# Quarter slots in native float32 for expert remainders of at most 32 tokens, beside 15 full slots

## The chip, the cores and the metric

The kernel runs on one core of a Trainium2 chip. The metric is the device time of one execution in microseconds, the median of several runs. A core has five engines with a queue each: PE (TensorE, matrix products), DVE (VectorE), ACT (ScalarE), POOL (GpSimd) and SP (SyncE, which here only reads control values and issues DMAs). An engine works through its own queue in order and waits on semaphores.

## The reference

Three stages follow each other. Attention with a sigmoid gives a matrix x of 1792 tokens by 768. A mixture of experts sends each token to one of eight experts, by the largest logit. A dense pair of layers with a squared relu ends it.

```python
# attention: 4 batches, 12 heads, 448 positions, 64 per head
attn = 1.0 / (1.0 + np.exp(-(scale * q @ k.T - np.log(S))));  x = attn @ v     # x: 1792 x 768
# experts: w1 is 8 x 768 x 1024, w2 is 8 x 1024 x 768
logits = x @ w_gate
expert_idx = np.argmax(logits, axis=1)
for e in range(8):
    mask = expert_idx == e
    out[mask] = gate_w[mask, None] * (np.maximum(x[mask] @ w1[e], 0.0) @ w2[e])
# dense: w_in is 768 x 2048, w_out is 2048 x 768
h = np.maximum(out @ w_in, 0.0);  result = h * h @ w_out
```

## The kernel before

All numbers are float32. Large products are made of two halves, a high part `h` rounded to the matmul's reduced float32 and the rest `l`: `mm3` issues three matmuls, high by high, high by low and low by high (lines 473 to 476). Attention's second product and the transposes are native float32 matmuls. In attention, two heads of 64 columns run as two column groups of the array, one after the other in program order (line 164).

**Routing** (lines 302 to 345) stands between attention and the experts. DVE finds each token's expert, PE counts tokens per expert and ranks them (`pn`, `prk`), and DVE rounds each count up to a multiple of 128 (`sa`), sums them up (`sx`) and so gives each token a position in a list of slots of 128 rows. `ctl[:,0]` holds the expert of each slot, `ctl[:,1]` whether it differs from that of the slot before (expert 0 for slot 0), `ctl[:,2]` the first row of the slot's result. A product with one-hot matrices (`A`, `Bt`) turns the positions into `idx`, the token of each row of each slot.

**The expert stage** (lines 434 to 640) runs `NBASE` slots, 19, whatever the routing; two more stand in a conditional block behind it. A slot gathers 128 rows of x (`gather`, an indirect DMA on POOL), transposes and splits them (`xtrans`), and goes through eight chunks of weights of 128x1536 (768 KB). Chunks 0 to 3 are `up` (36 matmuls of 512 columns in all), chunks 4 to 7 `down` (48 of 384), with two transposes of the hidden rows (`htrans`) between, and `fin` scales the result by the gate and stores it in `y_d`, with the token's number in a last column.

Weights go through three places. SP loads raw chunks: `reload(s, c)` is a DMA under the condition that the slot's expert differs from the one before, else it is skipped. The raw buffers are filled with expert 0's chunks at the end of attention. ACT then makes the high part `mh[c]` and DVE (POOL for chunk 7) the low part `ml[c]` (`split_m`). `next_chunk(s, c)`, called right after chunk c's matmuls, splits chunk c for slot s+1 and issues `reload(s+2, c)`. So PE is a slot behind the splits and two behind the loads.

The order on each engine is that of the program, written out by hand. For slot 0 the string `FIRST` (line 49) gives it: `h` is a high part on ACT, `l` or `p` a low part on DVE or POOL with `reload(1, c)` behind, `x0` the transposes of slot 0's rows, `r0` the rest of the routing (`late_routing`: first rows, gates' parts `gp`, `Bg`). The gates are one more one-hot product (`gates`, 16 matmuls) after chunk 3 of slot 0, into the PSUM tile `px1` that the second half of the transposes of slot 1 also uses.

The dense stage loads the rows of `y_d` in blocks of 512, the first block during the last expert slots, and scatters its results by token number.

Of the kernel before, what the change touches and what calls it, by code (L numbers as in the profile page):

```python
# [21 lines left out]
NT = B * S  # L22
# [14 lines left out]
NBASE = NTL + 5  # L37
# [19 lines left out]
def moe_kernel(ctx: ExitStack, tc: tile.TileContext, qk, v, wg, wm, w2, out):  # L57
# [8 lines left out]
    y_d = dram.tile([NT + 128, YW], F32, name="y_d")  # L66
    w_d = dram.tile([128, 16, CH], F32, name="w_d")
# [7 lines left out]
    idx = const.tile([128, NSLOT], U32, name="idx")  # L75
    gts = const.tile([128, NSLOT], F32, name="gts")
    ctl = const.tile([128, 3, NSLOT], I32, name="ctl")
    idx2 = const.tile([128, NTL], U32, name="idx2")
    tok = const.tile([128, NSLOT], U32, name="tok")
# [27 lines left out]
    with ExitStack() as actx:  # L107
# [171 lines left out]
        sa, sx = rt([128, 2, 1 + E], "sa"), rt([128, 2, 1 + E], "sx")  # L279
# [5 lines left out]
        A, Bs, Bt = rt([CP, NR, 128], "A", F16), rt([CP, NR, NSLOT], "Bs", F16), rt([CP, NR, NSLOT], "Bt", F16)  # L285
        cmp, r0 = rt([128, NSLOT, E - 1], "cmp"), rt([128, NSLOT], "r0")
        dst_, dd = rt([128, E], "dst_"), rt([128, E - 1], "dd")
        gp, Bg = rt([CP, NR, 3], "gp", BF16), rt([CP, NR, 3, NSLOT], "Bg", BF16)
# [10 lines left out]
        for tile in (ohz[:, :, 0:1], seg[:, :, 0:1], sa[:, :, 0:1], esl[:, 0:1]):  # L299
            nc.gpsimd.memset(tile, 0.0)  # L300
# [18 lines left out]
        V.tensor_scalar(sa[:, 0, 1:], t30, TWO30, None, op0=ALU.subtract)  # L319
        V.tensor_tensor_scan(sx[:, 0], seg[:, 0, :E + 1], sa[:, 0], 0.0, op0=ALU.mult, op1=ALU.add)  # L320
        nc.scalar.activation(sa[:, 1, 1:], pn[:, :E], AF.Copy)
# [7 lines left out]
        V.tensor_copy(ctl[:, 0, :], esl[:, 1:])  # L329
        V.tensor_tensor(ctl[:, 1, :], esl[:, 1:], esl[:, :NSLOT], op=ALU.not_equal)  # L330
# [103 lines left out]
    with ExitStack() as mctx:  # L434
# [4 lines left out]
        ps_ht = mctx.enter_context(tc.tile_pool(name="ps_ht", bufs=1, space=PS, reuse_waits="tile"))  # L439
        ps_y = mctx.enter_context(tc.tile_pool(name="ps_y", bufs=1, space=PS, reuse_waits="tile"))  # L440
# [50 lines left out]
        def make_slot(s, xh, xl, weights):  # L491
            hr = mp.tile([128, 2, 512], F32, tag="hr", name=f"hr_{s}", bufs=1)
# [13 lines left out]
            def up(c):  # L506
# [10 lines left out]
                if c % 2 == 1:  # L517
                    nc.scalar.activation(hr[:, i, :], ps[i], AF.Relu)
# [21 lines left out]

        regs(0)
# [4 lines left out]
        def late_routing():  # L546
            V.tensor_tensor_scan(sx[:, 1], seg[:, 0, :E + 1], sa[:, 1], 0.0, op0=ALU.mult, op1=ALU.add)
# [11 lines left out]
            V.tensor_scalar(ctl[:, 2, :], r0, float(NT), None, op0=ALU.min)  # L559
            V.tensor_tensor(gr, gr, gp[:, :, 1], op=ALU.subtract)  # L560
            V.tensor_copy(gp[:, :, 2], gr)
            for i in range(3):
                nc.gpsimd.tensor_tensor(Bg[:, :, i, :], Bs, gp[:, :, i:i + 1].to_broadcast([CP, NR, NSLOT]), op=ALU.mult)
            for s in range(3):
                row0(s)

        def gates():
            pg = ps_x.tile([128, 4, 128], F32, tag="px1", name="pgt").rearrange("p a b -> p (a b)")
            for t in range(NR):
                nc.tensor.matmul(pg[:, :3 * NSLOT], A[:, t, :], Bg[:, t].rearrange("p a s -> p (a s)"), start=(t == 0), stop=(t == NR - 1))  # L570
            V.tensor_copy(gts, pg[:, :NSLOT])
            V.tensor_tensor(gts, pg[:, NSLOT:2 * NSLOT], gts, op=ALU.add)
            V.tensor_tensor(gts, pg[:, 2 * NSLOT:3 * NSLOT], gts, op=ALU.add)
# [13 lines left out]
        for s in range(NBASE):  # L587
# [16 lines left out]
            for c in range(4, 8):  # L604
# [6 lines left out]
                next_chunk(s, c)  # L611
                if last and c < 7:
# [10 lines left out]
        with tc.If(more < NT):  # L623
            for s in range(NBASE, NSLOT):
# [22 lines left out]
    ps_q = ctx.enter_context(tc.tile_pool(name="ps_q", bufs=1, space=PS, reuse_waits="tile"))  # L647
    for c in range(2, RING):
# [137 lines left out]
```

## Time and profile before

| | us |
|---|---|
| median of 3 runs (1061.55 to 1066.33) | 1066.06 |
| the profiled execution | 1062.08 |
| its span, first to last instruction | 1060.5 |
| PE busy | 1013.8 |
| ACT busy | 638.8 |
| DVE busy | 631.8 |
| POOL busy | 188.4 |

The profile is of one execution. Busy time is the time in which an engine had an instruction running, as a share of the span a mean over all stages. Matmuls overlap each other, so the durations of single matmuls add up to more than their busy time; how fast they run is read from the distance of their starts. Attention lasts until about 185 us, the expert stage from about 205 to 576, the dense stage from 579 to the end. The mean granted clock of TensorE was 0.984.

### The profile page before, as it was taken

How to read it: one execution, taken by the hardware profiler on the slowest of the kernel's cores; microseconds unless marked ns; L12 is line 12 of the kernel's file. 1: busy time of each engine (PE TensorE's matmuls, PEld its weight loads, DVE VectorE, ACT ScalarE, POOL GpSimd, SP SyncE). 2: the span in 40 equal slices, each digit the busy share in tenths (PEclk: the TensorE clock that was granted, in tenths of full speed). 3: DMA queues.
4: the chain of work that ended last, by engine and by line, in shares of the span. 5: the costliest groups of instructions: out<-in, count | busy, mean ns of one | idle time of the engine just before them, and what ended most of it. 6: DMA issues, size and time to landing. Idle time of an engine off the chain costs nothing. (4 is left out here: it accounts for less than half of the span.)

```text
span 1060.5 us, 14396 instructions
## 1 busy us (share of the span) xinstructions
PE 1013.8 (96%) x5502; PEld 857.5 (81%) x5502; DVE 631.8 (60%) x565; ACT 638.8 (60%) x757; POOL 188.4 (18%) x132
## 2 busy tenths in 40 slices
PE   7999999379999999999998999999999999999997
PEld 3555555268888888888887889998899988899997
DVE  3777775788888888888883567433331334323351
ACT  5666664658887888878883664335542255522761
POOL 0000000464253342533411000001000010000100
PEclk9999999689999999999999999999999999999999
DMA  8788988763078174416344547434332432422650
GB/s 281 260 294 298 321 289 295 265 272 134 31 263 303 45 283 170 143 46 218 139 164 151 178 179 260 148 98 128 111 124 95 129 129 90 149 90 90 203 185 30
DMA packets 50104, 187.80 MB, mean 177 GB/s; under 512 B 6576, under 2 KB 17328, under 8 KB 47984
## 3 DMA queue, kind: packets, MB, share of 16 engines
q1 hardware_dynamic: 33872, 155.52, 42.2%
q0 software_dynamic: 4944, 25.56, 6.3%
q10 hardware_dynamic: 11216, 5.75, 2.1%
q8 instruction: 45, 0.74, 0.3%
q14 instruction: 27, 0.22, 0.1%
HBM read 230.85 MB, written 31.47 MB: 247 GB/s over the span
## 5 line engine op out<-in xcount | busy, mean ns | idle before, releaser
L358 DVE TENSOR_TENSOR wl<-raw,wh 128x1536 fp32r<-128x1536 f32 x126 | 256.0, 2053 | 51.8 <-ACT wh L357 49.4
L357 ACT ACTIVATE wh<-raw 128x1536 fp32r<-128x1536 f32 x144 | 213.7, 1484 | 2.9 <-ACT wh L357 0.2
L358 DVE TENSOR_TENSOR wrl<-raw,wrh 128x1536 fp32r<-128x1536 f32 x43 | 75.6, 1758 | 135.4 <-ACT wrh L357 135.4
L476 PE MATMUL py<-wh,hl 128*128 128x384 f32 x304 | 104.9, 345 | 6.0 <-DVE hl L504 6.0
L158 ACT ACTIVATE a<-sc,bias_s 128x896 f32<-128x896 f32 x96 | 82.6, 912 | 44.7 <-PE sc L154 44.5
L474 PE MATMUL py<-wh,hh 128*128 128x384 f32 x304 | 106.9, 352 | 0.0
L475 PE MATMUL py<-wl,hh 128*128 128x384 f32 x304 | 103.3, 340 | 0.1
L714 PE MATMUL pq<-wrh,sh 128*128 128x384 f32 x296 | 100.0, 338 | 0.0
L358 POOL TENSOR_TENSOR wl<-raw,wh 128x1536 fp32r<-128x1536 f32 x18 | 63.9, 3551 | 202.0 <-ACT wh L357 202.0
L716 PE MATMUL pq<-wrh,sl 128*128 128x384 f32 x296 | 99.5, 336 | 0.0
L715 PE MATMUL pq<-wrl,sh 128*128 128x384 f32 x296 | 99.5, 336 | 0.0
L676 PE MATMUL pp<-yh,wrh 128*128 128x512 f32 (+1 forms) x264 | 96.0, 364 | 2.7 <-PEq L623 2.7
L677 PE MATMUL pp<-yl,wrh 128*128 128x512 f32 (+1 forms) x264 | 95.9, 363 | 0.0
L678 PE MATMUL pp<-yh,wrl 128*128 128x512 f32 (+1 forms) x264 | 95.8, 363 | 0.0
L357 ACT ACTIVATE wrh<-raw 128x1536 fp32r<-128x1536 f32 x43 | 63.8, 1484 | 52.5 <-PE pq L716 43.2
L474 PE MATMUL ph<-wh,xh 128*128 128x512 f32 x228 | 92.7, 406 | 0.3 <-ACT xh L460 0.3
L476 PE MATMUL ph<-wh,xl 128*128 128x512 f32 x228 | 90.7, 398 | 0.0
L475 PE MATMUL ph<-wl,xh 128*128 128x512 f32 x228 | 90.6, 398 | 0.0
L680 ACT ACTIVATE r<-pp 128x512 f32<-128x512 f32 (+1 forms) x64 | 34.7, 542 | 86.3 <-PE pp L678 86.3
L358 DVE TENSOR_TENSOR rl<-raw,rh 128x1536 fp32r<-128x1536 f32 x21 | 36.9, 1758 | 75.8 <-ACT rh L357 75.8
L476 PEld LDWEIGHTS py<-wh,hl 128*128 128x128 f32 x304 | 57.8, 190 | 11.5 <-DVE hl L504 11.5
L164 PE MATMUL po<-a,qkv 128*64 128x448 f32 x288 | 64.7, 556 | 0.0
(168 smaller groups left out, 2045.7 us busy)
## 6 DMA issues: line engine op xcount, KB each, us to landing
raw<-in_wm SPq DMA_DIRECT2D x160, 768.0 KB
raw<-w_d SPq DMA_DIRECT2D x62, 768.0 KB
cs<-in_w SPq DMA_DIRECT2D x11, 1536.0 KB
qkv<-in_qk SPq DMA_DIRECT2D x23, 480.0 KB
w_d<-cd POOLq DMA_DIRECT2D x11, 768.0 KB, 9.6
raw<-in_w SPq DMA_DIRECT2D x5, 1536.0 KB
y_d<-y SPq DMA_DIRECT2D x19, 384.5 KB
qkv<-in_v SPq DMA_DIRECT2D x24, 256.0 KB
```

Of the source, the lines that this page charges most:

```text
L158: nc.scalar.activation(a[:, :n], ps[:, :n, :S], AF.Sigmoid, bias=bias_s, scale=1.0 / math.sqrt(D))
L357: nc.scalar.activation(h, src, AF.Copy)
L358: (nc.gpsimd if pool else nc.vector).tensor_tensor(l, src, f32(h), op=ALU.subtract)
L474: nc.tensor.matmul(ps, lh, rh, start=first, stop=False)
L475: nc.tensor.matmul(ps, lh, rl, start=False, stop=False)
L476: nc.tensor.matmul(ps, ll, rh, start=False, stop=last)
L676: nc.tensor.matmul(pp[:, :N], lh, rh, start=(k == 0), stop=False)
L677: nc.tensor.matmul(pp[:, :N], lh, rl, start=False, stop=False)
L678: nc.tensor.matmul(pp[:, :N], ll, rh, start=False, stop=(k == KD - 1))
L714: nc.tensor.matmul(po[t][:, :384], lh, wc[:, o:o + 384], start=(g == 0), stop=False)
L715: nc.tensor.matmul(po[t][:, :384], lh, wcl[:, o:o + 384], start=False, stop=False)
L716: nc.tensor.matmul(po[t][:, :384], ll, wc[:, o:o + 384], start=False, stop=(g == KF2 - 1))
```

## The change

An expert's tokens beyond its full slots, where they are at most 32, no longer get a slot of 128. Up to four such remainders go to quarter slots of 32 rows. The loop of full slots has 15 turns instead of 19, with six in the conditional block behind it. Each quarter is cut in ten events, and `q_due` puts event k right after the chunk with the number 8 + 5k/2, counted over all slots. An event is either a set of transposes (0 and 5) or one chunk of weights, used raw as float32: four column groups of 32, each with its own quarter of the chunk's columns. The weights of a quarter come through two buffers of their own (`qraw`, `QB` = 2), loaded on SP without condition. Routing gets the counts and positions for it, and slot 0 may start with another expert than 0. Some buffers become single: `xh`, `xl`, `hr` (now half as large), `y`, and the PSUM tile `pht`.

```diff
-NBASE = NTL + 5
+NBASE = NTL + 1
+NQ = 4
+QM = 32
+NCOL = NSLOT + NQ
+QB = 2
...
-        V.tensor_scalar(sa[:, 0, 1:], t30, TWO30, None, op0=ALU.subtract)
+        V.tensor_scalar(full, t30, TWO30, None, op0=ALU.subtract)
+        V.tensor_scalar(t30, pn[:, :E], 63.5 - QM, TWO30, op0=ALU.add, op1=ALU.add)
+        V.scalar_tensor_tensor(cand, t30, -TWO30, full, op0=ALU.add, op1=ALU.subtract)
+        V.tensor_tensor_scan(qs[:, 1:], seg[:, 0, 1:E + 1], cand, 0.0, op0=ALU.mult, op1=ALU.add)
+        V.scalar_tensor_tensor(t30, qs[:, 1:], -128.0 * NQ, cand, op0=ALU.is_ge, op1=ALU.mult)
+        V.tensor_tensor(sa[:, 0, 1:], full, t30, op=ALU.add)
         V.tensor_tensor_scan(sx[:, 0], seg[:, 0, :E + 1], sa[:, 0], 0.0, op0=ALU.mult, op1=ALU.add)
+        V.scalar_tensor_tensor(dlt, qs[:, :E], -128.0 * NSLOT, sx[:, 0, 1:], op0=ALU.add, op1=ALU.add)
...
+        V.tensor_tensor(posB, prk3, sa[:CP, 0, 1:].unsqueeze(2).to_broadcast([CP, E, NR]), op=ALU.is_ge)
+        V.tensor_tensor(posB, posB, dlt[:CP].unsqueeze(2).to_broadcast([CP, E, NR]), op=ALU.mult)
+        V.tensor_tensor(posA, posA, posB, op=ALU.subtract)
...
-            xh = mp.tile([128, KD, 128], F32R, tag="xh", name=f"xh_{s}")
-            xl = mp.tile([128, KD, 128], F32R, tag="xl", name=f"xl_{s}")
+            xh = mp.tile([128, KD, 128], F32R, tag="xh", name=f"xh_{s}", bufs=1)
+            xl = mp.tile([128, KD, 128], F32R, tag="xl", name=f"xl_{s}", bufs=1)
...
-            y = mp.tile([128, DM + 1], F32, tag="y", name=f"y_{s}")
+            y = mp.tile([128, DM + 1], F32, tag="y", name=f"y_{s}", bufs=1)
...
-                pt = ps_ht.tile([128, 4, 128], F32, tag=f"pht{i}", name=f"pht_{s}_{i}")
+                pt = ps_ht.tile([128, 4, 128], F32, tag="pht", name=f"pht_{s}_{i}")
...
+        def q_gather(q):
+            qx[q] = mp.tile([128, DM], F32, tag="qx", name=f"qx_{q}", bufs=1)
+            nc.gpsimd.indirect_dma_start(out=qx[q][:QM], out_offset=None, in_=x_d[:, :],
+                                         in_offset=bass.IndirectOffsetOnAxis(ap=idx[:QM, NSLOT + q:NSLOT + q + 1], axis=0))
+
+        def q_load(n):
+            q, c = n // 8, QORD[n % 8]
+            if q >= NQ:
+                return
+            if n % 8 == 0:
+                qe[q] = nc.sync.value_load(ctl[0:1, 0, NSLOT + q:NSLOT + q + 1], min_val=0, max_val=E - 1)
+            qr[n] = mp.tile([128, CH], F32, tag="qraw", name=f"qraw{n}", bufs=QB)
+            nc.sync.dma_start(out=qr[n], in_=wm[ds(qe[q], 1), :, c].rearrange("a p n -> (a p) n"))
+
+        def q_event(k):
+            q, e = divmod(k, 10)
+            if e == 0:
+                qt[0] = ps_q.tile([128, 512], F32, tag="q", name=f"qa_{q}")
+                for j in range(KD):
+                    nc.tensor.transpose(qt[0][:, QM * j:QM * j + QM], qx[q][:QM, j * 128:(j + 1) * 128], ident[:QM, :QM])
+                qt[1] = mp.tile([128, 256], F32, tag="qT", name=f"qxT_{q}", bufs=1)[:, :KD * QM].rearrange("p (a b) -> p a b", a=KD)
+                nc.scalar.activation(qt[1].rearrange("p a b -> p (a b)"), qt[0][:, :KD * QM], AF.Copy)
+                if q + 1 < NQ:
+                    q_gather(q + 1)
+            elif e < 5:
+                n = 8 * q + e - 1
+                c = QORD[n % 8]
+                w = qr.pop(n)
+                o = KD * QM + (c // 2) * 128
+                for i in range(3):
+                    kk = 3 * (c % 2) + i
+                    for j in range(4):
+                        nc.tensor.matmul(qt[0][QM * j:QM * j + QM, o:o + 128], qt[1][:, kk, :], w[:, i * 512 + 128 * j:i * 512 + 128 * j + 128],
+                                         start=(kk == 0), stop=(kk == KD - 1), skip_group_check=True, tile_position=(0, QM * j))
...
+                q_load(n + QB)
+            elif e == 5:
...
+                for i in range(2):
+                    nc.tensor.transpose(qt[0][:, i * 128:i * 128 + 128], qt[2][:, i, :], ident)
...
+            else:
...
+                for f in range(4):
+                    for j in range(4):
+                        nc.tensor.matmul(qt[0][QM * j:QM * j + QM, o:o + 96], qt[3][:, fg, QM * f:QM * f + QM], w[:, f * 384 + 96 * j:f * 384 + 96 * j + 96],
+                                         start=(fg == 0 and f == 0), stop=(fg == 1 and f == 3), skip_group_check=True, tile_position=(0, QM * j))
+                if e == 9:
...
+                    for j in range(4):
+                        nc.sync.dma_start(out=yq_d[q, :, :DM].rearrange("t (a j c) -> t a j c", a=2, j=4)[:, :, j, :], in_=yq[QM * j:QM * j + QM])
+                q_load(n + QB)
...
+        def quarters():
+            q_rows = srow[:, :NQ].unsqueeze(2).to_broadcast([128, NQ, E])
+            V.tensor_tensor(cmq, q_rows, qs[:, 1:].unsqueeze(1).to_broadcast([128, NQ, E]), op=ALU.add)
...
+        q_due = {}
+        for k in range(10 * NQ):
+            q_due.setdefault(8 + k * 5 // 2, []).append(k)
...
                 up(c)
                 next_chunk(s, c)
+                if s == 0 and c == 1:
+                    quarters()
+                    q_gather(0)
                 if s == 0 and c == 3:
                     gates()
...
+                    for n in range(QB):
+                        q_load(n)
+                q_step(s, c)
...
+        for q in range(NQ):
+            qrow[q] = nc.gpsimd.value_load(ctl[0:1, 2, NSLOT + q:NSLOT + q + 1], min_val=0, max_val=NT)
+            nc.gpsimd.dma_start(out=y_d[ds(qrow[q], QM), :DM + 1], in_=yq_d[q, :, :DM + 1])
```

## Rows read from the trace of the kernel before

**Rows 1.** The page: busy time of PE, and the chain that ended last by engine.
```profile
PE 1013.8 (96%) x5502; PEld 857.5 (81%) x5502; DVE 631.8 (60%) x565; ACT 638.8 (60%) x757; POOL 188.4 (18%) x132
...
PE 45%; POOLq 0%; issue 0%; ACT 0%
```

**Rows 2.** Windows of slots: bounds, length; PE, PEld, DVE, ACT, POOL busy; clock, DMA share, GB/s.
```profile
205.07:233.51 28.44, 22.48 (x114) 19.73 (x115) 26.78 (x32) 17.73 (x18) 18.02 (x7) 0.84 0.70 268
233.51:252.42 18.91, 18.56 (x99) 16.49 (x99) 15.94 (x11) 15.55 (x17) 7.54 (x3) 1.00 0.66 260
252.42:271.37 18.95, 18.60 (x99) 16.52 (x99) 16.00 (x11) 15.56 (x17) 7.54 (x3) 1.00 0.13 42
...
309.26:328.20 18.94, 18.59 (x99) 16.52 (x99) 16.00 (x11) 15.54 (x17) 7.54 (x3) 1.00 0.98 367
...
555.55:578.67 23.12, 20.43 (x117) 18.30 (x117) 10.38 (x13) 11.50 (x19) 4.15 (x6) 1.00 0.51 180
```

**Rows 3.** Timeline of PE, slot 0: start, length, instruction [idle before, releaser].
```profile
205.07 0.79 PE L474 MATMUL ph<-wh,xh 128*128 128x512 f32 x1 [0.26 <-ACT xh L460]
...
216.37 0.66 PE L570 MATMUL pgt<-Bg,A 112*128 112x63 bf16 x16 [1.15 <-POOL Bg L563]
216.87 0.42 PE L474 MATMUL py<-wh,hh 128*128 128x384 f32 x1
...
227.24 0.66 PE L459 MATMUL px<-ident,xg 128*128 128x128 f32 x2 [4.76 <-DVE gts L573]
```

**Rows 4.** Windows: the dense stage, columns as in rows 2.
```profile
578.67:1060.50 481.83, 474.60 (x2556) 437.79 (x2556) 185.25 (x166) 221.37 (x307) 20.69 (x29) 0.99 0.40 134
```

**Rows 5.** Timeline of PE in attention: column groups (128*64) and full width (128*128).
```profile
98.87 0.37 PE L154 MATMUL sc<-qkl,qkh 64*128 64x448 f32 x2
99.07 0.37 PE L154 MATMUL sc<-qkh,qkl 64*128 64x448 f32 x2
99.37 1.73 PE L164 MATMUL po<-a,qkv 128*64 128x448 f32 x8
101.03 0.47 PE L154 MATMUL sc<-qkh 64*128 64x448 f32 x2
...
102.54 0.91 PE L167 MATMUL po<-a,qkv 128*128 128x448 f32 x2
103.29 0.97 PE L177 MATMUL pt<-iw,xT 128*112 128x136 f32 x7
```

**Rows 6.** Timeline of PE in the slot from 309.26: end of up, transposes of the next rows.
```profile
318.12 0.34 PE L474 MATMUL py<-wh,hh 128*128 128x384 f32 x1
...
323.38 0.82 PE L459 MATMUL px<-ident,xg 128*128 128x128 f32 x6
323.95 0.42 PE L474 MATMUL py<-wh,hh 128*128 128x384 f32 x1
```

**Rows 7.** Timeline of DVE: routing, and the splits in slot 0.
```profile
189.45 0.17 DVE L319 TENSOR_SCALAR sa<-t 128x8 f32<-128x8 f32 x1
189.73 0.18 DVE L320 TENSOR_TENSOR_SCAN sx<-seg,sa 128x9 f32<-128x9 bf16 x1
...
212.29 3.41 DVE L358 TENSOR_TENSOR wl<-raw,wh 128x1536 fp32r<-128x1536 f32 x2
...
216.23 10.34 DVE L358 TENSOR_TENSOR wl<-raw,wh 128x1536 fp32r<-128x1536 f32 x2
```

**Rows 8.** Timeline of SP's DMA issues: slot 0's skipped reloads, a real one, one in a loading slot.
```profile
193.09 2.78 SPq L451 DMA_DIRECT2D raw<-in_wm  x8
...
197.42 0.34 SPq L451 DMA_DIRECT2D raw<-in_wm  x1
...
322.29 0.33 SPq L451 DMA_DIRECT2D raw<-in_wm  x1
```

**Rows 9.** Windows: the half microsecond in which the bytes of that real issue began.
```profile
198.00:198.50 0.50, 0.00 (x0) 0.00 (x0) 0.50 (x1) 0.50 (x1) 0.28 (x1) 0.50 1.00 123
```

**Rows 10.** Timeline of ACT: the copies of slot 0's transposed rows, 512 and 256 columns.
```profile
204.42 0.87 ACT L460 ACTIVATE xh<-px 128x512 fp32r<-128x512 f32 x2 [4.17 <-PE px L459]
```

More of the change, by code (lines that the diff above doesn't have):

```diff
@@ L74, in moe_kernel @@
     nc.scalar.activation(warm, bias_s, AF.Sigmoid)
-    idx = const.tile([128, NSLOT], U32, name="idx")
-    gts = const.tile([128, NSLOT], F32, name="gts")
-    ctl = const.tile([128, 3, NSLOT], I32, name="ctl")
+    idx = const.tile([128, NCOL], U32, name="idx")
+    gts = const.tile([128, NCOL], F32, name="gts")
+    ctl = const.tile([128, 3, NCOL], I32, name="ctl")
     idx2 = const.tile([128, NTL], U32, name="idx2")
-    tok = const.tile([128, NSLOT], U32, name="tok")
+    tok = const.tile([128, NCOL], U32, name="tok")
     wide = w2.dtype != F32
@@ L284, in moe_kernel @@
         posi, sli, pli = (rt([CP, NR], n, I32) for n in ("posi", "sli", "pli"))
[L285 removed]
+        A, Bs, Bt = rt([CP, NR, 128], "A", F16), rt([CP, NR, NCOL], "Bs", F16), rt([CP, NR, NCOL], "Bt", F16)
         cmp, r0 = rt([128, NSLOT, E - 1], "cmp"), rt([128, NSLOT], "r0")
         dst_, dd = rt([128, E], "dst_"), rt([128, E - 1], "dd")
[L288 removed]
+        gp, Bg = rt([CP, NR, 3], "gp", BF16), rt([CP, NR, 3, NCOL], "Bg", BF16)
+        full, cand, dlt, rows_q = (rt([128, E], n) for n in ("full", "cand", "dlt", "rows_q"))
+        qs, posB = rt([128, 1 + E], "qs"), eq.rearrange("p t e -> p (t e)").rearrange("p (e t) -> p e t", e=E)
+        cmq, rq_, beyond = rt([128, NQ, E], "cmq"), rt([128, NQ], "rq_"), rt([128, NSLOT], "beyond")
         iota(iot, [[1, 128]])
@@ L298, in moe_kernel @@
         nc.gpsimd.memset(seg, 1.0)
-        for tile in (ohz[:, :, 0:1], seg[:, :, 0:1], sa[:, :, 0:1], esl[:, 0:1]):
+        for tile in (ohz[:, :, 0:1], seg[:, :, 0:1], sa[:, :, 0:1], esl[:, 0:1], qs[:, 0:1]):
             nc.gpsimd.memset(tile, 0.0)
@@ L341, in moe_kernel @@
         for t in range(NR):
-            nc.tensor.matmul(pr[:, :NSLOT], A[:, t, :], Bt[:, t], start=(t == 0), stop=(t == NR - 1))
-        V.tensor_copy(idx, pr[:, :NSLOT])
-        V.tensor_scalar(tok, pr[:, :NSLOT], 128.0, 0.0, op0=ALU.subtract, op1=ALU.max)
+            nc.tensor.matmul(pr[:, :NCOL], A[:, t, :], Bt[:, t], start=(t == 0), stop=(t == NR - 1))
+        V.tensor_copy(idx, pr[:, :NCOL])
+        V.tensor_scalar(tok, pr[:, :NCOL], 128.0, 0.0, op0=ALU.subtract, op1=ALU.max)
         nc.scalar.activation(ez, z, AF.Exp)
@@ L558, in late_routing @@
             V.tensor_copy(gp[:, :, 1], gr)
-            V.tensor_scalar(ctl[:, 2, :], r0, float(NT), None, op0=ALU.min)
+            V.tensor_scalar(beyond, r0, sx[:, 1, E:E + 1], float(NT), op0=ALU.is_ge, op1=ALU.mult)
+            V.tensor_tensor(r0, r0, beyond, op=ALU.add)
+            V.tensor_scalar(ctl[:, 2, :NSLOT], r0, float(NT), None, op0=ALU.min)
             V.tensor_tensor(gr, gr, gp[:, :, 1], op=ALU.subtract)
@@ L569, in gates, with q_step @@
             for t in range(NR):
[L570 to L573, printed above, removed]
+                nc.tensor.matmul(pg[:, :3 * NCOL], A[:, t, :], Bg[:, t].rearrange("p a s -> p (a s)"), start=(t == 0), stop=(t == NR - 1))
+            V.tensor_copy(gts, pg[:, :NCOL])
+            V.tensor_tensor(gts, pg[:, NCOL:2 * NCOL], gts, op=ALU.add)
+            V.tensor_tensor(gts, pg[:, 2 * NCOL:3 * NCOL], gts, op=ALU.add)
+            for j in range(4):
+                nc.gpsimd.dma_start(out=gq[QM * j:QM * j + QM], in_=gts[:QM, NSLOT:])
+        q_due = {}
+        for k in range(10 * NQ):
+            q_due.setdefault(8 + k * 5 // 2, []).append(k)
+        def q_step(s, c):
+            for k in q_due.get(8 * s + c, ()):
+                q_event(k)
         xs = {}
@@ L611, in moe_kernel @@
                 next_chunk(s, c)
+                q_step(s, c)
                 if last and c < 7:
```

54 lines of the change are left out of this document (42 added, 12 removed).

## The prediction

> **What bounds the kernel now.** I read the page first, then the busy time of each engine in one window per slot, then TensorE's own timeline. On the page TensorE is busy for 96% of the span, and the chain that ended last is all but wholly PE [rows 1]. That share is a mean, so the stage of the change has to be read alone. The expert stage is 19 slots. The windows run from the first ph matmul of a slot to that of the next. From the second on they are 18.91 to 18.96 us long, 17 of them, of which I show three: one with little DMA traffic (42 GB/s), one with some (260) and one at 367 GB/s and a DMA share of 0.98. PE is busy for 18.6 us in each, ACT for 15.5, DVE for 16.0 [rows 2]. A slot that costs the same with the DMA engines idle and full is bound by TensorE. Slot 0 is the exception: 28.44 us, with PE stopped for 1.15 us until POOL's Bg and for 4.76 us until DVE's gts [rows 3], and a mean granted clock of 0.84 [rows 2]. The dense stage after it is 481.8 us, PE busy for 474.6 [rows 4]; the change only moves it.
>
> **What goes.** Worked out from the reference's inputs, the eight experts get 25, 19, 434, 5, 260, 235, 456 and 358 tokens. In slots of 128 that is 1+1+4+1+3+2+4+3 = 19, the number that the stage runs. Remainders of at most 32 are four: experts 0, 1, 3 whole and 4 tokens of expert 4. Full slots left: 4+2+2+4+3 = 15, exactly the new loop, so the conditional slots behind it stay empty and each of the four quarter slots is used. Four slots of 18.95 us go: **-75.8 us**.
>
> **What the quarter slots cost TensorE.** A quarter is 48 up matmuls of 128 columns, 64 down matmuls of 96 columns (both f32, 32 output rows, four column groups), six transposes of 32 rows and two full ones, in ten events put between chunks. Nothing before runs four column groups. The nearest rows are attention's f32 products [rows 5]. Full width, two matmuls of 448 columns take from 102.54 to 103.29: 0.375 us each, 0.84 ns a column. In two column groups eight of them, four pairs, take from 99.37 to 101.03: 0.39 us a pair, less the switch below. So two groups cost what one does, and f32 at 0.84 ns a column makes 0.107 us of 128 columns and 0.080 of 96. Entering that form costs about 0.09 us: 0.30 from 99.07 to 99.37 where 0.20 is usual (98.87 to 99.07). Seven matmuls of 136 columns with 112-column weights took 0.97 us, at most 0.139 each, so short f32 ones keep near their column price. Instructions have a floor too: the gate matmuls, 16 with a weight load each, started 0.50 us before what followed, 0.031 each [rows 3].
> - An up event of 12: the larger of 3 x 0.107 = 0.32 and 12 x 0.031 = 0.37, plus 0.18 for switching in and out: 0.55.
> - A down event of 16: the larger of 4 x 0.080 = 0.32 and 16 x 0.031 = 0.50, plus 0.18: 0.68.
> - Transposes: six full ones took 0.57 us [rows 6]; I take that plus 0.18 for the narrow ones and 0.19 for the two others: 0.94.
> - A quarter: 4 x 0.55 + 4 x 0.68 + 0.94 = 5.9; four: **+23.4 us**.
> Bounds: with no floor and no switching 8 x 0.32 + 0.4 = 3.0 a quarter, 12 in all. With the four groups one after another an event is 12 x 0.107 or 16 x 0.080 = 1.28, plus 0.18, so 12.6 a quarter, 50 in all. I stay near the two-group row, as it is the same mechanism at half the count.
>
> The Trainium skill, FP8 and Floating Point Precision, section TensorE Precision Notes, says that true fp32 takes four passes through the array. By it a column would cost 1.67 ns at 2.4 GHz; attention's rows show 0.84, two cycles, so the measurement decides. By the page's passes the quarters would be some 6.6 us dearer (an estimate).
>
> **What moves into the start.** Attention fills the raw buffers with expert 0's weights, and slot 0's conditional reload was a skip: eight issues went by in 2.78 us [rows 8]. Expert 0 has no full slot now; slot 0 belongs to expert 2, and all eight chunks of 768 KB must be read after routing. Step by step:
> - DVE gets five more dependent operations on [128x8] and three or four on [112x128] ahead of ctl. Neighbours there start 0.2 to 0.28 apart [rows 7]: +2.0 us for ctl and for the gather's idx.
> - The first reload then leaves SP at 193.1 + 2.0 = 195.1. Of an issue at 197.42 the first bytes moved in the window from 198.0 [rows 8, 9], 0.8 later; at 367 GB/s [rows 2] a chunk takes 2.1. Chunk k lands near 198.0 + 2.1k; chunk 4 near 206.4.
> - ACT is in order, and the list has h4 ahead of x0: two conversions of about 1.5 us may follow landings before xh, which began at 204.42 [rows 10]. Now it begins near 208.4, and the first ph near 209 instead of 205.07: +4.0. Later chunks land faster than PE's 2.4 us a chunk, so they cost nothing more; if the queue shares its rate with the gather they would, up to the whole load, 8 x 2.1 = 17.
> - Slot 0's own stops are tied to DVE and POOL. quarters() puts eight small operations, about 1.8 us, into DVE's queue ahead of the gts that PE waited for; Bg and the gates grow by 25/21, about 1.3 us on POOL. Both push the stops back: +3.0.
> Sum **+7 us** (from -3, if the shift takes slot 0's DVE split out of POOL's way: two splits took 10.34 us there and two others 3.41 [rows 7]; to +17).
>
> **What is hidden.** ACT gains four copies of 192 or 256 columns a quarter; copies of 512 and 256 took 0.87 together [rows 10], so under 0.5 each and 0.6 us a slot, against 3.4 idle [rows 2]. The single buffers of xh, xl, hr, y and the transposes are written well after their last readers in PE's order; y alone waits for its own store, with POOL's copy and the next gather behind it, and the gather has a slot to spare. If that cover went, a gather late by more than a slot would stop PE at chunk 5. The stores of quarters to y_d run on POOL behind the loop; the dense stage reads those rows only in its later blocks. SP takes 32 more loads and 16 small stores; the loads matter: the load for event n+2 is issued behind chunk c's reload, once event n is through PE. In a loading slot, up's last chunk ended at 318.12 and its reload left SP at 322.29 [rows 6, 8]: a lag of 4.2. With 0.8 and 2.1 that is 7.1 us, against five chunks and two events, 13 us. In the four slots that load a new expert (12 chunks at most, 25 us of DMA in 20) some loads are late: I take **+2 us** (0 to 13).
>
> **Sum.** The profiled run took 1062.08 us, span 1060.5: 1062.1 - 75.8 + 23.4 + 7 + 2 = 1018.7. That run lies 4 us under the median shown (1066.06; runs from 1061.55 to 1066.33), so I put the time at 1020.
>
> **Rivals.**
> - *The four column groups don't overlap*: quarters at 50 instead of 23.4. For it: no row has four groups. Against: two overlap fully. 1020 + 27 = 1047. Chance 0.13.
> - *Weight loads late in the loading slots*: 13 loads, a microsecond each, beside a longer start (+17 instead of +7): 1020 + 11 to 21, say 1036. For it: two buffers only and a DMA share of 0.98 in such a slot already; against: a new expert comes in four slots and none of them follow each other. Chance 0.14.
> - *Twice the column price* in these narrow forms: an up event at 3 x 0.214 + 0.18 = 0.82, a down event the same, so 4 x (0.27 + 0.14) more a quarter and 6.6 in all: 1020 + 6.6 = 1027. Attention's two column groups speak against it. Chance 0.03. The rule of the Trainium skill weighed above would give this.
> - *Slower*: every one of the 32 weight events stops PE because SP, in order, issues the load too late. It decides from (75.8 - 23.4 - 7) / 32 = 1.4 us an event; two loads are in flight, so landing must take 13 + 2.8 = 15.8 us instead of 7.1, as with four more chunks ahead of each. At 1.8 us an event: 1020 - 2 + 58 = 1076. Against: outside four slots the queue is nearly empty (42 GB/s). Chance 0.05.
> - *Not what it says*: an expert's remainder served by a conditional full slot after all, 1020 + 25 = 1045 with its loads uncovered. The counts speak against it. Chance 0.03.
>
> My forecast has 0.62, its own range 1010 to 1031. With the serial groups and the late loads inside, the range is 1008 to 1047. About 0.5%, 5 us, is what a measurement can tell here from no change: faster 0.92, within 0.03, slower 0.05.
>
> **What would show it.** Slots after the first at 18.95 us plus 0.6 to 0.7 per event; 3.3 events a slot, so near 20.8. The 12 matmuls of an up event starting within 0.45 us. PE's first ph near 209, and slot 1 near 240.5. Dense beginning near 535 and lasting 482. Wrong would be: events over 1.3 us, PE idle ahead of quarter matmuls waiting for DMA, or slot 0 over 40 us.

## The result, and the profile after

The changed kernel takes 1026.8 us (median of 4 runs, 1025.39 to 1029.55) against 1064.55 (4 runs, 1061.55 to 1066.33): a ratio of 0.9651, 95% interval 0.9618 to 0.9684. The forecast was 1020, its own range 1010 to 1031. The sign, the place and the time hold; three terms of the sum don't. The quarters' price rests on a misread row, the start on a stop that was taken for a possible gain, and the late loads were put too high.

The profiled execution took 1027.07 us. From the page of the kernel after: the span, the busy time of the engines, the first line of the chain that ended last, and attention's f32 products, which come back below.

```profile
span 1025.6 us, 15378 instructions
...
PE 972.7 (95%) x6038; PEld 815.1 (79%) x6038; DVE 569.8 (56%) x541; ACT 582.5 (57%) x709; POOL 151.7 (15%) x134
...
PE 46%; POOLq 0%; issue 0%; ACT 0%
...
L169 PE MATMUL po<-a,qkv 128*64 128x448 f32 x288 | 64.7, 556 | 0.0
```

PE still ends the chain and has lost 41.1 us of busy time (1013.8 in [rows 1]), 6.1 us more than the run did: some of what went was given back as idle time. The windows of the kernel after say where: slot 0, slots 1 and 2, the longest of the later slots, the last slot, the dense stage (columns as in rows 2).

```profile
212.38:245.77 33.39, 23.60 (x114) 20.93 (x115) 30.03 (x43) 17.80 (x18) 19.55 (x14) 0.74 0.24 85
245.77:267.65 21.88, 21.88 (x178) 18.57 (x177) 16.82 (x12) 16.54 (x20) 9.37 (x4) 1.00 0.27 83
267.65:288.20 20.55, 20.55 (x161) 17.93 (x157) 15.17 (x12) 16.12 (x19) 7.42 (x3) 1.00 0.82 315
...
351.18:374.14 22.96, 22.30 (x228) 18.95 (x227) 17.61 (x12) 17.11 (x19) 7.68 (x3) 1.00 0.66 261
...
520.36:543.47 23.11, 20.46 (x117) 18.39 (x117) 10.39 (x13) 11.55 (x19) 4.17 (x6) 1.00 0.48 160
543.47:1025.60 482.13, 474.18 (x2556) 437.37 (x2556) 185.20 (x166) 221.53 (x307) 23.32 (x33) 0.99 0.40 135
```

Three things are to be seen. The last slot and the dense stage are what they were, 23.11 and 482.13 us against 23.12 and 481.83 [rows 2, 4]. Slot 0 is 33.39 us instead of 28.44, and it begins at 212.38 instead of 205.07. And the slots with quarter events are longer, while PE in most of them no longer stands still at all (20.55 of 20.55 us). Against the profiled run of before, the sum is now: four slots, -75.8; slot 1 begins at 245.77 instead of 233.51, **+12.3**; the 13 slots from there to 520.36 take 274.59 us instead of 13 x 18.944 = 246.3 (17 slots from 233.51 to 555.55 [rows 2]), **+28.3**. That makes -35.2, with the dense stage's 0.3 some -34.9, and -35.0 was measured (1062.08 to 1027.07).

### The profile page after: what moved, and what is told of

It reads as the page before. It is cut to its first block, busy times and chain, and to the rows that moved or that the text cites. A ratio compares the mean times of both kernels' runs of the same rounds, so it can differ in the third digit from the quotient of the medians.

```text
span 1025.6 us, 15378 instructions
## 1 busy us (share of the span) xinstructions
PE 972.7 (95%) x6038; PEld 815.1 (79%) x6038; DVE 569.8 (56%) x541; ACT 582.5 (57%) x709; POOL 151.7 (15%) x134
## 5 line engine op out<-in xcount | busy, mean ns | idle before, releaser
L375 DVE TENSOR_TENSOR wl<-raw,wh 128x1536 fp32r<-128x1536 f32 x98 | 196.4, 2009 | 69.1 <-ACT wh L374 66.2
L374 ACT ACTIVATE wh<-raw 128x1536 fp32r<-128x1536 f32 x112 | 166.6, 1488 | 7.7 <-PE ph L494 6.0
L494 PE MATMUL py<-wh,hl 128*128 128x384 f32 x240 | 82.2, 342 | 9.8 <-DVE hl L522 9.8
L492 PE MATMUL py<-wh,hh 128*128 128x384 f32 x240 | 85.9, 358 | 0.0
L493 PE MATMUL py<-wl,hh 128*128 128x384 f32 x240 | 81.9, 341 | 0.0
L492 PE MATMUL ph<-wh,xh 128*128 128x512 f32 x180 | 75.5, 420 | 4.7 <-ACT xh L478 4.7
L375 POOL TENSOR_TENSOR wl<-raw,wh 128x1536 fp32r<-128x1536 f32 x14 | 49.1, 3508 | 162.9 <-ACT wh L374 162.9
L494 PE MATMUL ph<-wh,xl 128*128 128x512 f32 x180 | 71.5, 397 | 0.0
L493 PE MATMUL ph<-wl,xh 128*128 128x512 f32 x180 | 71.5, 397 | 0.0
L169 PE MATMUL po<-a,qkv 128*64 128x448 f32 x288 | 64.7, 556 | 0.0
L799 PEld LDWEIGHTS pp<-yh,wrh 128*128 128x128 f32 x264 | 50.2, 190 | 10.5 <-issue 2.9
```

Source lines behind the costliest of these rows:

```text
L374: nc.scalar.activation(h, src, AF.Copy)
L375: (nc.gpsimd if pool else nc.vector).tensor_tensor(l, src, f32(h), op=ALU.subtract)
L492: nc.tensor.matmul(ps, lh, rh, start=first, stop=False)
L493: nc.tensor.matmul(ps, lh, rl, start=False, stop=False)
L494: nc.tensor.matmul(ps, ll, rh, start=False, stop=last)
L799: nc.tensor.matmul(pp[:, :N], lh, rh, start=(k == 0), stop=False)
```

## The experiments

Each ratio is to the kernel before, run on the same chip, with a 95% interval. "Slot 1" is the time of its first ph matmul in the profiled run: 233.51 before, 245.77 after. Diffs are against the kernel after unless said otherwise.

### by_group: the column groups one after the other

```
-                for i in range(3):
-                    kk = 3 * (c % 2) + i
-                    for j in range(4):
+                for j in range(4):
+                    for i in range(3):
+                        kk = 3 * (c % 2) + i
...
-                for f in range(4):
-                    for j in range(4):
+                for j in range(4):
+                    for f in range(4):
```

> The same quarter matmuls, ordered by column group: all of group 0, then group 1, and so on, so that at most one pair at a border can run side by side. Theory (four groups run side by side in the changed kernel, an event's matmuls start within 0.6 us): each f32 matmul is two passes of 0.107 us (128 columns) or 0.080 (96), so an event's body becomes 4 x 6 x 0.107 = 2.6 us less up to 0.3 of overlap at the borders, and the time 1027 + 32 x 1.6 to 2.0 = 1078 to 1090, slower than the kernel before. Rival (one pass a matmul, as the prediction's bound had it): body 1.28, time near 1048. Rival (groups never overlapped): no change, 1027.

Measured: 1051.41 us, ratio 0.9888 (0.9865 to 0.9911). None of the three numbers was met; 1048 comes nearest, but its one pass a matmul is not what the rows show. An up event on PE's timeline, in the kernel after (start, length, instruction):

```profile
252.94 0.40 PE L494 MATMUL ph<-wh,xl 128*128 128x512 f32 x1
253.27 0.86 PE L599 MATMUL qa<-qraw,qxT 128*32 128x128 f32 x24
254.06 0.50 PE L492 MATMUL ph<-wh,xh 128*128 128x512 f32 x1
```

And the same event with the groups in sequence:

```profile
251.39 0.39 PE L494 MATMUL ph<-wh,xl 128*128 128x512 f32 x1
251.71 1.59 PE L599 MATMUL qa<-qraw,qxT 128*32 128x128 f32 x24
253.22 0.50 PE L492 MATMUL ph<-wh,xh 128*128 128x512 f32 x1
```

The same 24 instructions take 1.59 instead of 0.86 us. The 13 slots behind slot 0 take 302.34 us instead of 274.59, so 27.8 more, 0.87 for each of the 32 weight events; the timed run takes 24.6 more (24.2 in the profiled one, where slot 1 began 1.6 us earlier and what follows the 13 slots was 2.0 shorter; why, these runs don't show). So the order side by side is worth 0.87 us an event, and the four groups do overlap in the kernel after: its single instructions start four at a time, 7 ns apart, and the next four start 0.11 us after these (0.13 the first time). Even in sequence they are not serial. 24 rows at 0.107 us would be 2.57 (an estimate); so some of the next group's instructions ran beside the last of the group before. A fully serial form was not run.

The row also shows something else: x24 where the program has 12 matmuls.

### loads_only: the events without their arithmetic

```
-                qt[0] = ps_q.tile([128, 512], F32, tag="q", name=f"qa_{q}")
-                for j in range(KD):
-                    nc.tensor.transpose(...)
...
-                        nc.tensor.matmul(qt[0][QM * j:QM * j + QM, o:o + 128], ...)
...
+            elif e != 5:
+                n = 8 * q + e - 1 - (e > 5)
+                qr.pop(n)
...
+                    nc.gpsimd.memset(yq.rearrange("p a b -> p (a b)"), 0.0)
```

The events keep their loads and their stores, without matmuls, transposes or copies; the four remainders' tokens are not computed.

> The quarter events keep their weight loads and stores but no matmul, transpose or copy (zeros are stored as the quarters' results), so the tokens of the four remainders are not computed. Theory (the events' cost is TensorE's own time, the loads stop PE for under 1 us in all): slots after the first at 18.95 us, time 27 to 28 us lower, 998 to 1000. Rival (the loads and stores slow the slots through the DMA queues and SP's order): slots at 19.3 or more where an expert is loaded, time over 1004.

Measured: 1003.25 us, ratio 0.9434 (0.9403 to 0.9465). The window of the 13 slots behind slot 0, and that of one of them:

```profile
244.44:491.39 246.95, 242.07 (x1275) 215.61 (x1275) 207.68 (x143) 202.73 (x209) 89.30 (x45) 1.00 0.70 258
...
263.44:282.45 19.01, 18.62 (x100) 16.60 (x100) 15.98 (x11) 15.60 (x17) 7.52 (x3) 1.00 0.81 294
```

The same 13 slots in the kernel after:

```profile
245.77:520.36 274.59, 273.93 (x2204) 236.94 (x2203) 204.47 (x143) 207.35 (x225) 88.17 (x41) 1.00 0.65 234
```

A slot with the loads alone is back at 18.97 to 19.01 us, even at 294 GB/s, and the 13 slots take 246.95 us. So the quarters' arithmetic is worth 274.59 - 246.95 = 27.6 us, and 32 loads and 16 stores together 0.7 (246.95 - 246.3). PE is busy 31.9 us longer with the arithmetic (273.93 against 242.07), but it stands still for 0.7 us instead of 4.9: without the arithmetic the stop for hl is there again, 13 times, 4.9 us in all. The time itself lies 3 to 5 us above the theory's, and the slots are not the reason: the dense stage took 486.4 us here, with this stop of PE in its first matmuls and a granted clock of 0.50 behind it (PE's timeline):

```profile
518.08 0.58 PE L769 MATMUL pp<-yh,wrl 128*128 128x512 f32 x1 [3.16 <-issue]
```

What the engine waited for there, the trace does not say; it stays open.

### prefetch2: attention loads the first full slot's expert

```
-                    nc.sync.dma_start(out=raw[c], in_=wm[0, :, len(raw) + c])
+                    nc.sync.dma_start(out=raw[c], in_=wm[2, :, len(raw) + c])
...
+        nc.gpsimd.memset(esl[:, 0:1], 2.0)
```

Slot 0's reload is a skip again, as before the change. That slot 0 belongs to expert 2 is known here from the inputs; this is a probe, not a kernel for any routing.

> Attention's prefetch loads expert 2's weights instead of expert 0's, and the first reload is conditional on that, so slot 0's load is covered again. Theory (the uncovered load is the larger part of the longer start): first ph at 207 to 208 instead of 212.4, slot 1 at 240 to 241.5 instead of 245.8, time 1021 to 1023. Rival (slot 1 is set by the collision of DVE's and POOL's splits and by the added DVE operations, the load is hidden behind that): first ph moves, slot 1 less than 2 us, time 1025 to 1027.

Measured: 1020.6 us, ratio 0.9597 (0.9569 to 0.9625). PE's timeline of slot 0 in the kernel after:

```profile
206.20 1.51 PE L477 MATMUL px<-ident,xg 128*128 128x128 f32 x6 [8.33 <-DMA xg<-x_d,idx]
212.38 0.80 PE L492 MATMUL ph<-wh,xh 128*128 128x512 f32 x1 [4.67 <-ACT xh L478]
...
233.80 0.69 PE L494 MATMUL py<-wh,hl 128*128 128x384 f32 x1 [9.78 <-DVE hl L522]
...
245.77 0.39 PE L492 MATMUL ph<-wh,xh 128*128 128x512 f32 x1
```

And with expert 2 prefetched:

```profile
202.72 1.51 PE L478 MATMUL px<-ident,xg 128*128 128x128 f32 x6 [4.59 <-DMA xg<-x_d,idx]
204.50 0.79 PE L493 MATMUL ph<-wh,xh 128*128 128x512 f32 x1 [0.26 <-ACT xh L479]
...
228.35 0.69 PE L495 MATMUL py<-wh,hl 128*128 128x384 f32 x1 [8.53 <-DVE hl L523]
```

DVE's timeline with expert 2 prefetched, ahead of hl:

```profile
215.17 10.95 DVE L376 TENSOR_TENSOR wl<-raw,wh 128x1536 fp32r<-128x1536 f32 x2
```

The gather lands 3.5 us earlier, ACT's wait before the first ph is gone, and slot 1 begins at 240.06, 5.7 us earlier. That is what the forced reload costs beside the change's other edits. The stop for hl stays at 8.53 us, so the reload is not needed for it, and slot 1 is still 6.6 us later than before (240.06 against 233.51): so much the other edits cost with the load covered.

### before_no_prefetch: the reload alone, in the kernel before

Against the kernel before:

```
-        for tile in (ohz[:, :, 0:1], seg[:, :, 0:1], sa[:, :, 0:1], esl[:, 0:1]):
+        for tile in (ohz[:, :, 0:1], seg[:, :, 0:1], sa[:, :, 0:1], ):
...
+        nc.gpsimd.memset(esl[:, 0:1], float(E))
```

Slot 0 must read its expert again, though it is in the buffers.

> The kernel before, with slot 0's reloads forced, so that all eight chunks of its first expert are read after routing, as the changed kernel must. Nothing else of the change is in it. Theory (the uncovered load costs 5 to 7 us by itself): first ph about 5 us later than 205.1, slot 1 at 238 to 241 instead of 233.5, time 1067 to 1070 where the kernel before has 1062.4. Rival (the added routing operations and quarters make the start longer, not the load): 1062 to 1064.

Measured: 1068.21 us, ratio 1.0042 (1.0022 to 1.0063); slot 1 at 241.68, 8.2 later. PE's timeline of its slot 0:

```profile
210.87 0.79 PE L475 MATMUL ph<-wh,xh 128*128 128x512 f32 x1 [6.16 <-ACT xh L461]
...
229.68 0.69 PE L477 MATMUL py<-wh,hl 128*128 128x384 f32 x1 [6.73 <-DVE hl L505]
```

The first ph comes 5.8 us late without any of the change's other edits, and the stop for hl appears with it. So the reload alone is enough to bring both; prefetch2 shows that the other edits alone are enough to bring the stop. The two parts, 8.2 and 6.6, are more than the 12.3 together, so they can't be added up. The timed runs show 4.6 us, less than the profile's 8.2.

### x0_early: the rows ahead of two conversions on ACT

```
-FIRST = "h0 l0 h1 l1 h2 l2 h3 p3 h4 x0 l4 r0 h5 p5 h6 l6 h7 p7"
+FIRST = "h0 l0 h1 l1 h2 l2 x0 h3 p3 h4 l4 r0 h5 p5 h6 l6 h7 p7"
```

> The transposes of slot 0's rows come ahead of h3 and h4 in the hand-written order. Theory (ACT's place in its queue delays PE's first matmul, but slot 1 is set by DVE's chain from l4 on, which waits for chunk 4 as before): first ph near 208 instead of 212.4, the stop for hl in slot 0 longer by as much, slot 1 within 1 us of 245.8, time 1026 to 1028. Rival (PE's first start sets what follows): slot 1 near 241.5, time near 1023.

Measured: 1026.27 us, ratio 0.9644 (0.9617 to 0.9672). PE's timeline:

```profile
207.76 0.79 PE L492 MATMUL ph<-wh,xh 128*128 128x512 f32 x1 [0.26 <-ACT xh L478]
...
233.55 0.69 PE L494 MATMUL py<-wh,hl 128*128 128x384 f32 x1 [8.59 <-DVE hl L522]
```

PE starts 4.6 us earlier, stops 3.3 us for ACT's hr on the way, and reaches hl's first matmul at the same time as after (233.55, 233.80). My 4.0 us for the first ph was a real delay, but not one that ended last.

### dve_splits and quarters_late: what holds hl

In dve_splits two splits go from POOL to DVE:

```
-FIRST = "h0 l0 h1 l1 h2 l2 h3 p3 h4 x0 l4 r0 h5 p5 h6 l6 h7 p7"
+FIRST = "h0 l0 h1 l1 h2 l2 h3 p3 h4 x0 l4 r0 h5 l5 h6 l6 h7 l7"
```

> Slot 0's low parts of chunks 5 and 7 are made by DVE instead of POOL (two operations of 1.75 us more for DVE, POOL's 6.85 us gone). Theory (DVE's two splits of 10.9 us in slot 0 are slowed by POOL's running beside them): they take 3.5 us, hl comes 3 to 4 us earlier, slot 1 at 241.5 to 243, time 1023 to 1024.5. Rival (the splits are slow for another reason): hl 3.5 us later, slot 1 near 249, time 1030.

In quarters_late the planning of the quarters goes behind the gates:

```
-                    quarters()
...
+                    quarters()
```

> The eight small operations of quarters() stand behind the gates in slot 0 instead of ahead of the split of chunk 2. Theory (PE's stop in slot 0 ends with hl, at the end of DVE's chain, and these operations are 1.6 us of it): hl and slot 1 1.5 us earlier, time 1024.5 to 1025.5. Rival (something else ends the stop at the same time): slot 1 within 0.5 us of 245.8, time 1026 to 1027.

Measured: dve_splits 1022.0 us, ratio 0.962 (0.9593 to 0.9647), slot 1 at 239.98, 5.8 earlier; quarters_late 1024.37, ratio 0.9628 (0.9598 to 0.9657), slot 1 at 243.54, 2.2 earlier. DVE's timeline in slot 0 of the kernel after, with hl at 233.06:

```profile
220.67 10.90 DVE L375 TENSOR_TENSOR wl<-raw,wh 128x1536 fp32r<-128x1536 f32 x2
231.49 0.18 DVE L659 TENSOR_TENSOR cmq<-srow,qs 128x32 f32<-128x32 f32 x1
...
232.93 0.23 DVE L666 TENSOR_SCALAR ctl<-rq__1687,sx 128x4 int32<-128x4 f32 x1
233.06 0.68 DVE L522 TENSOR_TENSOR hl<-pht,hh 128x512 fp32r<-128x512 f32 x1
233.66 3.42 DVE L375 TENSOR_TENSOR wl<-raw,wh 128x1536 fp32r<-128x1536 f32 x2
```

POOL's timeline beside it:

```profile
219.08 2.39 POOL L653 TENSOR_TENSOR Bg<-Bs,gp 112x400 bf16<-112x400 f16 x1 [0.62 <-DVE gp L651]
221.43 6.85 POOL L696 TENSOR_TENSOR wl<-raw,wh 128x1536 fp32r<-128x1536 f32 x2
```

And DVE's timeline in dve_splits, with the first pair ahead of hl and the second behind it:

```profile
223.78 3.41 DVE L375 TENSOR_TENSOR wl<-raw,wh 128x1536 fp32r<-128x1536 f32 x2
...
229.22 3.42 DVE L375 TENSOR_TENSOR wl<-raw,wh 128x1536 fp32r<-128x1536 f32 x2
```

Two splits take 10.90 us on DVE beside POOL's, which run until 228.28, and 3.41 without them. hl stands behind them in DVE's queue, with the quarters' small operations (231.49 to 233.16, 1.7 us) between, and PE waits 9.78 us for it. In dve_splits PE still waits 6.1 us for hl, with two more splits ahead of it in that queue. The Trainium skill, SBUF — State Buffer, section SBUF: two separate sides, calls the port pair that the two engines share an exclusive lock: an operation of DVE with two SBUF inputs and one of GpSimd that reads SBUF shut each other out for a whole instruction. The trace agrees, 10.90 against 3.41 us.

### before_dve_splits: the same edit in the kernel before

Against the kernel before:

```
-FIRST = "h0 l0 h1 l1 h2 l2 h3 p3 h4 x0 l4 r0 h5 p5 h6 l6 h7 p7"
+FIRST = "h0 l0 h1 l1 h2 l2 h3 p3 h4 x0 l4 r0 h5 l5 h6 l6 h7 l7"
```

> The kernel before with chunks 5 and 7 of slot 0 split by DVE instead of POOL. Theory (the collision of the two engines' splits costs the kernel before some microseconds too): DVE's 10.3 us for two splits become 3.5, slot 1 at 229 to 231 instead of 233.5, time 2 to 4 us under the kernel before. Rival (only the changed kernel is held by it): no change.

Measured: 1060.87 us, ratio 0.9968 (0.9951 to 0.9986); slot 1 at 231.84, 1.7 earlier. The two splits take 3.41 us there too (10.34 in [rows 7]), but PE then stops 4.46 us for POOL's Bg, where it stopped 4.76 for DVE's gts [rows 3]. So of the 5.8 us that dve_splits brings behind the change, 1.7 were there to be had before it; by the medians it is 2.7 of 4.8.

### start_order: three edits of the start together

```
+FIRST = "h0 l0 h1 l1 h2 l2 x0 h3 p3 h4 l4 r0 h5 l5 h6 l6 h7 l7"
...
-                next_chunk(s, c)
+                if s > 0:
+                    next_chunk(s, c)
+                elif c > 1:
+                    next_chunk(0, c - 2)
...
+                    quarters()
+                    next_chunk(0, 2)
+                    next_chunk(0, 3)
```

The rows and DVE's splits as above; slot 1's conversions come two chunks later, those of chunks 2 and 3 and the quarters' planning behind the gates.

> The start alone is reordered: x0 ahead of h3, chunks 5 and 7 split by DVE, slot 1's first two splits behind hl in DVE's queue, quarters() behind the gates. The events are those of the changed kernel. Theory (slot 1's start is set by DVE's chain up to hl; with that shortened PE's own start counts): the stop for hl falls from 9.8 us to 2 to 4, slot 1 at 234 to 237 instead of 245.8, time 1015 to 1018. Rival (the uncovered load then takes the place, chunks 5 to 7 arriving late): slot 1 at 239 or later, time 1020 or more.

Measured: 1021.28 us, ratio 0.9588 (0.9563 to 0.9614), slot 1 at 239.17. That is the rival's number, but not by its wait. PE's timeline:

```profile
216.79 0.66 PE L520 MATMUL pht<-ident,hr 128*128 128x128 f32 x4 [2.23 <-ACT hr L537]
...
224.34 0.45 PE L494 MATMUL py<-wh,hl 128*128 128x384 f32 x1 [1.52 <-DVE hl L522]
...
233.66 0.45 PE L494 MATMUL py<-wh,hl 128*128 128x384 f32 x1 [3.73 <-DVE hl L522]
```

One stop of 9.78 us became three, 7.5 in all: the splits that were put off now stand ahead of the second hl. Moving the same work about in DVE's queue gains little more than dve_splits alone (239.98).

### pairs and load_first: fewer entries, and the loads' place on SP

In pairs, the eight weight events of a quarter stand two and two at four places:

```
-            q_due.setdefault(8 + k * 5 // 2, []).append(k)
+            k_ = k + (k % 10 in (1, 3, 6, 8))
+            q_due.setdefault(8 + k_ * 5 // 2, []).append(k)
```

> The eight weight events of a quarter stand in pairs at four places instead of eight, the same matmuls and loads. Theory (each place costs about 0.28 us for going into and out of the narrow form beside the matmuls): 16 places fewer, 4 to 5 us less, time 1021.5 to 1023. Rival 1 (the cost is the matmuls' own): 1026 to 1027. Rival 2 (with two buffers the second load of a pair comes late): PE idle ahead of quarter matmuls, 1028 or more.

Measured: 1023.8 us, ratio 0.963 (0.9603 to 0.9657); the 13 slots take 273.59 us instead of 274.59. The time lies between the theory's and the rivals', and the second rival's stops are there. PE's waits for the quarters' weights in them (us in total, times, longest):

```profile
PE qb L619 <- DMA qraw<-in_wm: 2.1, 2, 1.1
PE qa L599 <- DMA qraw<-in_wm: 1.5, 2, 1.0
```

These four stops are 3.6 us, where the kernel after has one of 0.7. So the joined entries gave 1.0 + 3.6 - 0.7 = 3.9 us, and 2.9 of it went to the later loads. In load_first the event, and with it the next load, is also put ahead of the chunk's own reload on SP:

```
+                if s > 0:
+                    q_step(s, c)
...
-                q_step(s, c)
...
-                next_chunk(s, c)
...
+                next_chunk(s, c)
```

> The paired events once more, and on SP each quarter load stands ahead of its chunk's reload instead of behind it, so that it waits for the event's matmuls alone and not for the split. Theory (pairs saved 4.6 us in places and gave 3.6 back because the loads left SP some 4 us after the event): PE's four stops of 0.5 to 1.1 us for qraw go to under 0.5 in all, time 1020 to 1021. Rival (the loads are late because the DMA queues are full in the loading slots): the stops stay, 1023 to 1024.

Measured: 1020.24 us, ratio 0.9583 (0.9558 to 0.9607); the 13 slots take 269.2 us and no wait for these loads is left. SP's issues of the four loads that PE stopped for, first in pairs:

```profile
329.41 0.92 SPq L577 DMA_DIRECT2D qraw<-in_wm  x2
...
362.07 1.69 SPq L577 DMA_DIRECT2D qraw<-in_wm  x2
```

Then with the event ahead of the reload:

```profile
327.08 1.25 SPq L577 DMA_DIRECT2D qraw<-in_wm  x2
...
358.13 0.91 SPq L577 DMA_DIRECT2D qraw<-in_wm  x2
```

2.3 and 3.9 us earlier on SP is the difference between a stop and none.

### all_three: start_order, pairs and load_first

The edits of the three together.

> The reordered start, the paired events and the earlier loads together. Theory (the gains lie in different stretches and add up): 1010 to 1013. Rival (loads of the first pairs come late because slot 1 starts earlier): 1014 to 1017.

Measured: 1014.65 us (1012.9 to 1016.65), ratio 0.9528 (0.9503 to 0.9553): it beats both kernels. It misses the theory's range and lies in the rival's, but not by the rival's wait: PE stops for the quarters' weights once, for 0.5 us. Slot 1 begins at 238.37 and the dense stage at 531.43, 12.0 earlier than after: 7.4 from the start and 4.6 from the slots.

## Why the prediction was right, and where it was not

**What goes**: right. 15 full slots ran, no conditional one, and the dense stage kept its length; "not what it says" is out.

**What the quarter slots cost TensorE**: 27.6 us (loads_only) instead of 23.4. The step that failed is "f32 at 0.84 ns a column". I took a row of the profile for a matmul of the program. An f32 product leaves two: L169 has x288 on the page for 144 products, and the events have as many as 384 and 512 rows for 192 and 256 (from the groups of lines of the expert stage of the kernel after; busy, mean ns, idle):

```profile
L619 PE MATMUL qb<-qraw,qhT 128*32 128x96 f32 x512 | 13.9, 249 | 0.7 <-DMA qraw<-in_wm 0.7
L599 PE MATMUL qa<-qraw,qxT 128*32 128x128 f32 x384 | 13.8, 277 | 0.0
```

Each row is a pass of 0.84 ns a column, so a column costs 1.67 ns, four cycles of 2.4 GHz. The rule of the Trainium skill that I weighed and set aside (FP8 and Floating Point Precision, section TensorE Precision Notes, four passes) was right, and I had read the trace against it wrongly. Its rival, 1027 us at a chance of 0.03, had the column price right, and its 6.6 us stand beside 4.2 measured (27.6 - 23.4). The two differ because something was given back.

From start to start an up event costs 254.06 - 252.94 = 1.12 us, less the 0.235 that the ph matmul would have taken: 0.88 where I said 0.55 (0.82 by that rival). A down event is the same. Two passes of its columns are 0.64 in either (6 x 0.107, 8 x 0.080), so switching in and out takes some 0.24 instead of 0.18; the prediction's floor of 0.031 us an instruction doesn't show, as four rows start 7 ns apart. 32 x 0.88 = 28.2, and with the prediction's own 4 x 0.94 for the transposes 32.0, an estimate beside the 31.9 us that PE is busy longer than in loads_only. Against it, the stop for hl of 0.35 us a slot, PE busy for 18.60 of 18.95 [rows 2], is gone (20.55 of 20.55), and loads_only has it back, 4.9 us in all. In the kernel after each of the 13 slots has an event ahead of the place where PE waited. In load_first two have none; the stop is back in one of these (0.4 us) and in no other slot. So the events standing ahead take the stop away, though not alone, as the second of the two shows. 31.9 - 4.9 + 0.7 (the one stop for a quarter's weights) = 27.7 beside the 27.6 measured. The prediction had no line for the stop. That the slots came near its 20.8 (20.55 and 21.88 above, 20.53 to 21.45 in most) is two errors that partly cancel.

**Four groups that don't overlap**: out. by_group shows what losing only part of the overlap costs, 27.8 us in the slots. With two passes a product this rival's 50 would have been some 92 (32 x (2.57 + 0.18) + 3.8, an estimate).

**The start**: +12.3 us instead of +7. The gather and xh were late as the steps had it, and more so (first ph at 212.38, forecast 209): ACT, in order, held xh behind h4, which waited for its chunk (ACT's timeline of the kernel after). The conversions of chunks 0 and 4 began at 199.88 and 210.36, so a chunk took 2.6 us where the steps had 2.1 (198.0 and 206.4).

```profile
199.88 1.48 ACT L690 ACTIVATE wh<-raw 128x1536 fp32r<-128x1536 f32 x1 [7.98 <-DMA raw<-in_wm]
...
210.36 1.48 ACT L690 ACTIVATE wh<-raw 128x1536 fp32r<-128x1536 f32 x1 [0.40 <-DMA raw<-in_wm]
211.75 0.85 ACT L478 ACTIVATE xh<-px 128x512 fp32r<-128x512 f32 x2
```

But x0_early shows that this delay is no term of the sum: taken away alone, it left slot 1 where it was. The steps that failed are the one that said later chunks "cost nothing more" and the +3.0 for slot 0's own stops: prefetch2 puts the load at 5.7 us and the other edits, with the load covered, at 6.6. In the kernel before, DVE's first pair of slot 1's splits went undisturbed, hl followed, and the second pair met POOL's (10.34 [rows 7]). DVE's timeline of the kernel before, between the two pairs:

```profile
215.63 0.68 DVE L504 TENSOR_TENSOR hl<-pht,hh 128x512 fp32r<-128x512 f32 x1
```

In the kernel after the first pair meets POOL's, and hl stands behind it. PE then stopped once for 9.78 us for hl, where it had stopped for 1.15 and 4.76 [rows 3]. The reload alone brings this (before_no_prefetch), and so do the other edits alone (prefetch2). The prediction had seen that DVE and POOL meet there and put it at "from -3", a gain. Removing the reload (5.7), or POOL's two splits (5.8), gives nearly the same; the two together were not tried, so how far the two gains overlap is open.

**What is hidden**: right on copies, stores and buffers; loads_only puts loads and stores at 0.7 us. Late loads cost one stop of 0.7 (L619 above) instead of 2, so "weight loads late" and "slower" are out. The lag by which the load on SP would matter was close, though: pairs needed two loads at once and had four stops.

**Sum**: -75.8 + 28.3 + 12.3 against -75.8 + 25.4 + 7, so the run gained 8.2 us less than forecast. Both large misses went the same way, and the range was wide enough for them. The rival's 1027 falls on the measured 1026.8 by luck: it had the quarters 2.4 us and the late loads 1.3 us too dear, and the start 5.3 us too short.

## What to carry to other kernels

Count the rows of an instruction against the program's own loops before a price is taken from them: a known total (here 144 products, 288 rows) is the test that a duration alone doesn't give. When a transfer at the head of a stage becomes later, follow it past the engine that reads it first, to the next engine's queue and whatever stands behind it there; the delay that ends last can be two engines away, and two edits can each be enough to bring it, so that taking one back doesn't remove it. And small work that is put into a stream that already waits is paid in part by that wait, so its price is to be taken against the slot's idle time and not on its own.

## What the runs showed of the hardware that was not expected

- The four column groups overlap in part even when each group's matmuls are issued in a run: 1.59 us for 24 rows, between 0.86 side by side and 2.57 in series (24 x 0.107, an estimate).
- The long stop in slot 0 costs more than itself. Windows of the kernel after, ahead of the stop, in it, and behind it (columns as in rows 2):

```profile
221.00:224.00 3.00, 3.00 (x27) 2.15 (x25) 3.00 (x1) 2.49 (x4) 3.00 (x2) 1.00 0.02 5
224.00:233.50 9.50, 0.02 (x1) 0.00 (x0) 9.27 (x11) 1.06 (x1) 9.04 (x5) 0.61 0.07 9
233.80:239.60 5.80, 5.80 (x19) 5.70 (x20) 4.44 (x6) 1.34 (x2) 1.69 (x4) 0.50 0.31 91
```

  The granted clock was 1.00 (2.4 GHz) with PE busy, and 0.50 (1.2 GHz) when PE came back after 9.78 us without work: the py matmuls behind it start 0.32 us apart, and 0.18 apart from 240 us on. The 5.8 us of work at half the clock are some 2.9 us longer than at the full one (an estimate). Slot 0's mean clock went from 0.84 [rows 2] to 0.74.
- Of DVE's two splits in 10.90 us the first took 9.2 and the second 1.7, by the trace's single instructions. The first ended at 229.90, 1.6 us after POOL's second split, about a split's own time: it had waited for both of POOL's. The engine that paid was PE, through hl's 0.68 us behind them.
